# K's and Q's weights loaded in four blocks of 2 KB pieces, and the first products taken block by block

## The chip, the cores and the metric

The kernel runs on one core of one Trainium2 chip. Its engines are TensorE (PE in the profile; its weight loads have a row of their own, PEld), VectorE (DVE), ScalarE (ACT), GpSimd (POOL) and SyncE (SP), which here only issues DMAs. The metric is device time in microseconds for one execution. A median over runs is given, and beside it one execution that was taken apart by the profiler.

## The reference

The input x has 2048 rows (tokens) of 512 numbers in bf16. It is normalised row by row, and two blocks are added to it: a linear attention with 32 heads of 16, and a SwiGLU layer of width 1792.

```python
xn = _layernorm(x, axis=-1)
return x + _A_ref(xn, A_wqkv, A_wo) + _B_ref(xn, B_w_gate, B_w_up, B_w_down)

# A:  q, k, v from xn @ wqkv           (wqkv is 512 x 1536: q, then k, then v)
phi = lambda t: jnp.where(t > 0, t + 1, jnp.exp(t)) + 1e-6
pq, pk = phi(q), phi(k)
kv = jnp.einsum("bhsd,bhse->bhde", pk, v)
z = jnp.einsum("bhsd->bhd", pk)
num = jnp.einsum("bhqd,bhde->bhqe", pq, kv)
den = jnp.einsum("bhqd,bhd->bhq", pq, z)[..., None] + 1e-6
o = num / den                          # then o @ wo
# B:  (silu(x @ w_gate) * (x @ w_up)) @ w_down
```

The attention has no mask and sums over all tokens, so it doesn't matter which token stands in which row of a tile as long as input and output agree.

## The kernel before, in words

The 2048 tokens are cut into 16 tiles of 128. A small class collects the instructions of each engine in a list, in the order in which the code calls them, and works out the waits from the names of what each reads and writes (`_Prog`, L25 on). So the order of work is written out by hand: each engine goes through its list strictly in the order of the calls. A DMA stands in the list of the engine that issues it, SP or ACT. One wait holds up everything behind it on that engine. Every DMA has a semaphore of its own.

The stages are these. First the tiles are normalised and K and Q are computed (`proj_part`, `proj_first`, `proj`), with phi on ACT and DVE. V is never computed: TensorE accumulates xn-transposed times phi(K) in four banks of its output memory over all tiles (`gtacc`, L620). Then comes the SwiGLU layer in 56 steps (`ffn`), with the attention's small products in between, and then, tile by tile, the output products (`out_mm`), one addition and the store.

The change touches the first ten microseconds. There the order is this:

- `fill` (L267, called L644 and L645) has TensorE multiply constants until the first x tile is there.
- The loads: x tiles by `xload` (L204), K's and Q's weights by `wqkv_load` (L210). The weight matrix has 512 rows, loaded as four blocks c = 0 to 3 of 128 rows, one row in each partition. K's part of a row is 512 numbers, 1 KB, and Q's another 1 KB right ahead of it. One call loads one block (or two) of K or of Q. Calls L250 to L262: SP issues x 0, K 0 and 1, K 2, x 2, Q 0, Q 1, x 3, Q 2, Q 3, x 4, x 5, x 6 and 7; ACT issues x 1 (L240) and K 3.
- `rows` (L199) says which rows of x make a tile. The first `NLONE` tiles are 128 rows following each other, one per partition. The rest are dealt out so that each partition holds neighbouring rows; a load of two such tiles then has pieces of 2 KB.
- Tiles 0 to 3 don't wait for the variance. Their rows less the mean (`xc_half`, `xc_act`, `xc_add`, `xc_full`: L377 to L430) are transposed and multiplied, and the scale `rstd` is applied to the product. Tiles 0, 1 and 2 are transposed on TensorE (`tp_block` L407, `tp_first` L439) and copied out of its output memory by ACT or DVE (`tc_block` L416, `tc_first` L452). Tile 3 goes by a transposing DMA (`transpose_xc`, L432), as do the later tiles (`transpose_dma`, L460).
- `proj_part(t, wname, c, pos)` (L495) is one matmul: block c of tile t times block c of K's or Q's weights. `pos` is its place among the four that add up to one result; the first starts the sum, the fourth ends it. It waits for the tile's block and for the weights' block c. `proj_first` (L481) does two blocks in one call.
- K of a tile that is complete goes to ACT: `first_ek` (L554, an exponential) and `first_pk` (L560, the positive part). DVE clips the exponential (`clip_k`, L592), and POOL or DVE adds the two (`feat_pool` L578, `first_feat` L585). Q goes through `first_pq` (L572).

K of tile t uses bank 2 * (t % 2), Q the bank after it, so tile 2's K product must wait until ACT has read tile 0's K, tile 2's Q until ACT has read tile 0's Q, and tile 3's until ACT has read tile 1's.

The order of the calls is in L644 to L768. Around the change TensorE's list is: transposes of tiles 0 and 1; K of tile 0 (blocks 0, 1, 3, 2); K of tile 1 (the same); Q of tile 1, blocks 0 and 1; Q of tile 0, blocks 0 and 1; transposes of tile 2; Q's blocks 2 and 3 for both tiles; then K and Q of tile 2, `gtacc(0)`, and tile 3. DVE's list from L668 on: statistics of tile 2, its two halves less the mean, statistics of tile 3, `clip_k(0)`, `xc_full(3)`, statistics of tiles 4, 5 and 6, `clip_k(1)`, `xn(4)`. SP's list behind the first loads: `transpose_xc(3)`, x 8 and 9, x 10 and 11, and then the transpose of tile 4.

Of the kernel before, what the change touches and what calls it, by code (L numbers as in the profile page):

```python
# [10 lines left out]
P = 128  # L11
S = 2048
D = 512
# [96 lines left out]
def bass_parallel_sum__linear_attn_block__swiglu_ffn__prompt_kernel(  # L110
# [12 lines left out]
    K = _Prog()  # L123
    pe, act, dve, pool, sp = nc.tensor, nc.scalar, nc.vector, nc.gpsimd, nc.sync
    bf, f32 = dt.bfloat16, dt.float32

    with contextlib.ExitStack() as es:
        E = es.enter_context

        def sb(name, shape, d=bf):  # L130
            return E(nc.sbuf_tensor(name, [P] + shape, d))
# [7 lines left out]
        wqkv_sb = sb("wqkv_sb", [NDC, 3 * D])  # L139
# [52 lines left out]
        def bk(i):  # L192
            return ("bank", i)

        NLONE = 6

        def rows(v, t0, n):  # L199
            if t0 < NLONE:  # L200
                return v[t0 * P:(t0 + n) * P, :].rearrange("(t p) d -> p t d", p=P)
            return v[NLONE * P:, :].rearrange("(p t) d -> p t d", t=NT - NLONE)[:, t0 - NLONE:t0 - NLONE + n, :]

        def xload(eng, h, t0, n, after=()):  # L204
            K.dma(
                eng, lambda: h.dma_start(x_sb[:, t0:t0 + n, :], rows(xin, t0, n)),
                r=list(after), w=[("x", t0 + i) for i in range(n)],
            )

        def wqkv_load(eng, h, name, i, c0, n, after=()):  # L210
            K.dma(
                eng,
                lambda: h.dma_start(
                    wqkv_sb[:, c0:c0 + n, i * D:(i + 1) * D],
                    A_wqkv[c0 * P:(c0 + n) * P, i * D:(i + 1) * D].rearrange("(c p) f -> p c f", p=P),
                ),
                r=list(after), w=[(name, c) for c in range(c0, c0 + n)],
            )

        def wload(eng, h, name, dst, src):  # L220
# [27 lines left out]
        )  # L248

        xload("sp", sp, 0, 1)  # L250
        wqkv_load("sp", sp, "wk", 1, 0, 2)
        wqkv_load("act", act, "wk", 1, 3, 1)
        wqkv_load("sp", sp, "wk", 1, 2, 1)
        xload("sp", sp, 2, 1)
        wqkv_load("sp", sp, "wq", 0, 0, 1)
        wqkv_load("sp", sp, "wq", 0, 1, 1)
        xload("sp", sp, 3, 1)
        wqkv_load("sp", sp, "wq", 0, 2, 1)
        wqkv_load("sp", sp, "wq", 0, 3, 1)
        xload("sp", sp, 4, 1)  # L260
        xload("sp", sp, 5, 1)
        xload("sp", sp, 6, 2)  # L262

        cw = nc.const_aps.tensor(1.0, (P, P), bf)
# [33 lines left out]
        def bns(t):  # L298
            K.op("dve", lambda: dve.bn_stats(stats[:, t, :], x_sb[:, t, :]), r=[("x", t)], w=[("st", t)])  # L299
# [23 lines left out]
        def eps(t, eng):  # L323
            h = dve if eng == "dve" else pool
            K.op(
                eng,
                lambda: h.tensor_scalar(
                    out=vpe[:, t:t + 1], in0=mv[:, t, 1:2], scalar1=1e-5, scalar2=None, op0=ALU.add,
                ),
                r=[("mv", t)], w=[("vpe", t)],  # L330
            )

        def rstd_of(t):
            K.op(
                "pool",
                lambda: pool.tensor_tensor(out=rstd[:, t:t + 1], in0=vpe[:, t:t + 1], in1=nhalf[:, 0:1], op=ALU.pow),
                r=[("vpe", t), ("nhalf",)], w=[("rstd", t)],
            )
# [93 lines left out]
        def transpose_xc(t):  # L432
            K.dma(
                "sp",
                lambda: sp.dma_start_transpose(out=xcT[:, NDC * t:NDC * (t + 1), :], in_=xc_sb[:, t, :]),
                r=[("xc", t, 0), ("xc", t, 1)], w=[("xcT", t, c) for c in range(NDC)],
            )

        def tp_first(t, h, b):  # L439
            tb = banks[b].bitcast(bf)[:, 0:HD].rearrange("p (c s) -> p c s", c=2)  # L440
            K.op(
                "pe",
                [
                    (lambda c=c: pe.transpose(  # L444
                        tb[:, c, :], xc_sb[:, t, (2 * h + c) * P:(2 * h + c + 1) * P], ident[:, :],
                    ))
                    for c in range(2)
                ],
                r=[("xc", t, h), ("ident",)], w=[bk(b)],
            )  # L450

        def tc_first(t, h, b):  # L452
            tb = banks[b].bitcast(bf)[:, 0:HD].rearrange("p (c s) -> p c s", c=2)
            K.op(
                "act",
                lambda: act.activation(xcT[:, NDC * t + 2 * h:NDC * t + 2 * h + 2, :], tb, ACT.Copy),
                r=[bk(b)], w=[("xcT", t, 2 * h), ("xcT", t, 2 * h + 1)],
            )
# [36 lines left out]
        def proj_part(t, wname, c, pos):  # L495
            lo, b = (D, kb(t)) if wname == "wk" else (0, qb(t))
            K.op(
                "pe",
                lambda: pe.matmul(  # L499
                    banks[b], xcT[:, NDC * t + c, :], wqkv_sb[:, c, lo:lo + D],  # L500
                    start=(pos == 0), stop=(pos == NDC - 1),
                ),
                r=[("xcT", t, c), (wname, c)], w=[bk(b)],
            )

        def kb(t):
            return 2 * (t % 2)

        def qb(t):
            return 2 * (t % 2) + 1  # L510
# [43 lines left out]
        def first_ek(t):  # L554
            K.op(
                "act", lambda: act.activation(ek[:, t % NE, :], banks[kb(t)], ACT.Exp, scale=rstd[:, t:t + 1]),
                r=[bk(kb(t)), ("rstd", t)], w=[("ek", t % NE)],
            )

        def first_pk(t):  # L560
            K.op(
                "act", lambda: act.activation(kpos[:, t % NE, :], banks[kb(t)], ACT.Relu, scale=rstd[:, t:t + 1]),
                r=[bk(kb(t)), ("rstd", t)], w=[("kpos", t % NE)],
            )
# [90 lines left out]
        tc_block(0, 0, 4, "dve")  # L655
        tc_block(0, 1, 5, "act")
        tp_first(0, 1, 6)
        tc_first(0, 1, 6)
        eps(0, "pool")
        tp_first(1, 0, 7)  # L660
        tp_first(1, 1, 3)
        tc_first(1, 0, 7)
        bns(1)
        rstd_of(0)
        xn_dve(0)
# [7 lines left out]
        agg(3)  # L673
        proj_part(0, "wk", 0, 0)
        proj_part(0, "wk", 1, 1)
        proj_part(0, "wk", 3, 2)
        proj_part(0, "wk", 2, 3)
        first_ek(0)
        clip_k(0)
        xc_full(3)  # L680
        bns(4)
        proj_part(1, "wk", 0, 0)
        proj_part(1, "wk", 1, 1)
        proj_part(1, "wk", 3, 2)
        proj_part(1, "wk", 2, 3)
        proj_part(1, "wq", 0, 0)
        proj_part(1, "wq", 1, 1)
        transpose_xc(3)
        xload("sp", sp, 8, 2)
        xload("sp", sp, 10, 2)  # L690
        proj_part(0, "wq", 0, 0)
        proj_part(0, "wq", 1, 1)
        first_pk(0)
        tp_first(2, 0, 4)
        tc_first(2, 0, 4)
# [428 lines left out]
```

## Time and profile before

| what | value |
|---|---|
| median of 3 runs | 210.37 us (210.27 to 211.07) |
| the profiled execution, device time | 210.88 us |
| its span in the profile | 209.6 us |
| moved by DMA | 16.84 MB, mean 80 GB/s |
| busiest engine after TensorE | DVE, 57% of the span |

The profile has one row for each group of instructions: start, time from the first start to the last end, engine, line of the kernel, operation, what is written from what, the count, and in brackets how long the engine stood idle before and what released it. A table by stretches gives for each stretch its length and each engine's busy time in it with the number of instructions (x...), in the order PE, PEld, DVE, ACT, POOL; then the granted clock of TensorE, the busy share of the DMA engines, and GB/s. The granted clock stands at 1.00 in all of them here; the beat at which matmuls start is a finer measure. A matmul's row is longer than the beat, because matmuls overlap.

### The profile page before, as it was taken

The numbers are of one execution on the slowest core, as the hardware profiler recorded it, in microseconds if no ns is written. First come the engines' busy times: TensorE is split into PE (matmuls) and PEld (weight loads), VectorE is DVE, ScalarE is ACT, GpSimd is POOL, SyncE is SP. The second block draws the span as 40 slices with busy tenths as digits, with TensorE's granted clock in tenths as the row PEclk, the third lists the DMA queues.
The fourth block names the chain that finished last, engine by engine and source line by source line (L and its number), as shares of the span: only waits on it lengthen the run. The fifth ranks groups of instructions, "written<-read, shape, count | busy, mean of one in ns | idle before, by whom it ended". The sixth has DMA issues, their size and how long they took to land.

```text
span 209.6 us, 2822 instructions
## 1 busy us (share of the span) xinstructions
PE 206.9 (99%) x1014; PEld 94.5 (45%) x1014; DVE 120.3 (57%) x246; ACT 71.3 (34%) x126; POOL 72.0 (34%) x90
## 2 busy tenths in 40 slices
PE   8999999999999999999999999999999999999996
PEld 3444444444444444444444444444444444444444
DVE  4989989335465874637355746365556535374122
ACT  6686666976543331302122312213031213121000
POOL 3526977658032443223141422240424132221200
DMA  6763644697797021010101110102011010110101
GB/s 201 225 179 71 127 78 100 175 377 240 192 359 68 2 46 26 29 25 25 50 2 50 28 25 25 50 0 53 2 48 25 27 28 25 46 32 25 50 28 50
DMA packets 30287, 16.84 MB, mean 80 GB/s; under 512 B 20928, under 2 KB 29632, under 8 KB 30272
## 3 DMA queue, kind: packets, MB, share of 16 engines
q1 hardware_dynamic: 29984, 16.39, 29.9%
q10 hardware_dynamic: 288, 0.26, 0.4%
q8 instruction: 8, 0.13, 0.3%
q14 instruction: 7, 0.06, 0.1%
HBM read 9.70 MB, written 2.10 MB: 56 GB/s over the span
## 4 chain that ended last, share of the span: by engine, by line
PE 97%; DMA 1%; DVE 1%; issue 0%
PE psum L821 46%; PE psum L1026 23%; PE psum L472 10%; PE psum L1015 7%; PE psum L624 7%; PE psum L499 2%; PE psum L486 2%; DMA x_sb<-in_A_x_dram 1%; PE psum L444 0%; DVE stats L299 0%; PE psum L928 0%; PE psum L410 0%; PE psum L951 0%; DVE xc_sb L380 0%; DVE out_sb L1039 0%
## 5 line engine op out<-in xcount | busy, mean ns | idle before, releaser
L836 ACT ACTIVATE sg<-psum 128x512 bf16<-128x512 f32 x56 | 33.4, 598 | 106.0 <-PE psum L821 103.6
L821 PE MATMUL psum<-xnT,wg_sb 128*128 128x512 bf16 x224 | 57.5, 379 | 0.0
L821 PE MATMUL psum<-xnT,wu_sb 128*128 128x512 bf16 x224 | 57.5, 379 | 0.0
L970 POOL TENSOR_TENSOR prod<-pkq,zb 128x512 f32<-128x512 bf16 x16 | 18.6, 1161 | 55.9 <-DVE pkq L548 55.9
L821 PEld LDWEIGHTS psum<-xnT,wu_sb 128*128 128x128 bf16 x224 | 21.9, 98 | 26.4
L821 PEld LDWEIGHTS psum<-xnT,wg_sb 128*128 128x128 bf16 x224 | 21.7, 98 | 26.2 <-issue 0.2
L1039 DVE TENSOR_TENSOR out_sb<-psum,x_sb 128x512 bf16<-128x512 f32 (+2 forms) x17 | 11.2, 660 | 35.9 <-PE psum L1026 35.9
L994 POOL TENSOR_TENSOR pqn<-pkq,rden 128x512 bf16<-128x512 bf16 x16 | 16.9, 1055 | 36.6 <-DVE rden L988 36.6
L842 DVE TENSOR_TENSOR pkq<-psum,sg 128x512 bf16<-128x512 f32 x28 | 19.2, 686 | 17.1 <-PE psum L821 14.7
L842 DVE TENSOR_TENSOR xn_sb<-psum,sg 128x512 bf16<-128x512 f32 x28 | 18.8, 671 | 14.2 <-PE psum L821 13.6
L1026 PE MATMUL psum<-wd_sb,xn_sb 128*128 128x512 bf16 (+2 forms) x126 | 25.7, 355 | 0.0
L1026 PE MATMUL psum<-wd_sb,pkq 128*128 128x512 bf16 x112 | 25.5, 379 | 0.0
L472 PE MATMUL psum<-wqkv_sb,xnT 128*128 128x512 bf16 x96 | 22.5, 379 | 0.0
L616 POOL TENSOR_TENSOR zacc<-zacc,pkq 128x512 f32<-128x512 f32 x15 | 17.3, 1155 | 5.0 <-DVE ek L539 4.6
L1026 PEld LDWEIGHTS psum<-wd_sb,xn_sb 128*128 128x128 bf16 x126 | 11.8, 98 | 12.5
L1026 PEld LDWEIGHTS psum<-wd_sb,pkq 128*128 128x128 bf16 x112 | 11.0, 98 | 13.2
L1015 PE MATMUL psum<-m_sb,eq 128*128 128x512 bf16 (+2 forms) x68 | 16.6, 366 | 0.0
L624 PE MATMUL psum<-pkq,xn_sb 128*128 128x512 bf16 x64 | 15.9, 379 | 0.0
L472 PEld LDWEIGHTS psum<-wqkv_sb,xnT 128*128 128x128 bf16 x96 | 9.4, 98 | 11.3
L978 DVE TENSOR_REDUCE den<-prod 128x32 f32<-128x512 f32 x16 | 10.9, 683 | 5.9 <-POOL prod L970 5.9
L299 DVE BATCH_NORM_STATS2 stats<-x_sb 128x6 f32<-128x512 bf16 x16 | 10.9, 679 | 3.3 <-DMA x_sb<-in_A_x_dram 3.3
L548 DVE SCALAR_TENSOR_TENSOR pkq<-pkq,eq 128x512 bf16<-128x512 bf16 x16 | 11.1, 693 | 0.6
(73 smaller groups left out, 139.3 us busy)
## 6 DMA issues: line engine op xcount, KB each, us to landing
out_dram<-out_sb SPq DMA_DIRECT2D x15, 128.0 KB, 1.7
wg_sb<-in_B_w_gate_dram SPq DMA_DIRECT2D x2, 896.0 KB, 8.2
wu_sb<-in_B_w_up_dram SPq DMA_DIRECT2D x2, 896.0 KB, 6.4
wd_sb<-in_B_w_down_dram SPq DMA_DIRECT2D x1, 1792.0 KB, 11.1
x_sb<-in_A_x_dram SPq DMA_DIRECT2D x5, 256.0 KB, 3.0
x_sb<-in_A_x_dram SPq DMA_DIRECT2D x5, 128.0 KB, 3.2
wqkv_sb<-in_A_wqkv_dram SPq DMA_DIRECT2D x5, 128.0 KB, 3.4
wqkv_sb<-in_A_wqkv_dram SPq DMA_DIRECT2D x1, 512.0 KB, 8.4
```

The lines of the kernel that those rows point to most:

```text
L472: (lambda c=c: pe.matmul(banks[b], xnT[:, c, t * P:(t + 1) * P], wqkv_sb[:, c, lo:lo + D], start=(c == 0), stop=(c == NDC - 1),))
L548: lambda: dve.scalar_tensor_tensor(out=dst, in0=src, scalar=0.0, in1=e, op0=ALU.max, op1=ALU.add,),
L616: lambda: pool.tensor_tensor(out=zacc[:, :], in0=zacc[:, :], in1=pk, op=ALU.add),
L624: (lambda c=c: pe.matmul(banks[4 + c], xn_sb[:, t, c * P:(c + 1) * P], pkq[:, t, 0, :], start=(t == 0), stop=(t == NT - 1),))
L821: (lambda c=c: pe.matmul(banks[b], w_sb[:, c, fc * P:(fc + 1) * P], xnT[:, c, C * 512:(C + 1) * 512], start=(c == 0), stop=(c == NDC - 1),))
L836: lambda: act.activation(sg[:, j % NSG, :], banks[gb], ACT.Silu),
L842: lambda: dve.tensor_tensor(out=hT(C, fc), in0=banks[ub], in1=sg[:, j % NSG, :], op=ALU.mult,),
L970: lambda: pool.tensor_tensor(out=p, in0=pkq[:, t, 1, :], in1=zb[:, :], op=ALU.mult),
L994: lambda: pool.tensor_tensor(out=pqn[:, t % NPN, :].rearrange("p (i g h e) -> p g i h e", i=NB, g=NG, e=DH), in0=pkq[:, t, 1, :].rearrange ...
L1015: (lambda g=g: pe.matmul(dst, pqnT(t)[:, g, :], m_sb[:, g, lo:hi], start=(g == 0), stop=False,))
L1026: (lambda fc=fc: pe.matmul(dst, hT(C, fc)[:, jj * P:(jj + 1) * P], wd_sb[:, fc, lo:hi], start=False, stop=(fc == NFC - 1),))
L1039: lambda: dve.tensor_tensor(out=o, in0=src, in1=x_sb[:, t, lo:hi], op=ALU.add),
```

## The change

K's and Q's weights of one block of rows lie side by side, so one load now takes both: 128 rows with pieces of 2 KB. There are four such loads in place of seven. Block 1 is issued by ACT, the others by SP. `NLONE` goes from 6 to 4, so x tiles 4 and 5 have the dealt-out rows, and one load takes both. Tiles 0 and 1 now take their products block by block: K for both tiles and Q for tile 0 with blocks 0 and 1, then K for both with blocks 2 and 3; Q of tile 1 with blocks 0 and 1 comes after that. So the K result of tile 0 is complete after nine products and not after four, that of tile 1 after ten and not after eight. `transpose_xc(3)` and the loads of x 8 to 11 keep their places in SP's list. The copy `tc_first(0, 1)` goes behind `tc_first(1, 0)` in ACT's list.

```diff
-        NLONE = 6
+        NLONE = 4
...
+        def qk_load(eng, h, c):
+            K.dma(
+                eng,
+                lambda: h.dma_start(wqkv_sb[:, c, 0:2 * D], A_wqkv[c * P:(c + 1) * P, 0:2 * D]),
+                w=[("wk", c), ("wq", c)],
+            )
...
         xload("sp", sp, 0, 1)
-        wqkv_load("sp", sp, "wk", 1, 0, 2)
-        wqkv_load("act", act, "wk", 1, 3, 1)
-        wqkv_load("sp", sp, "wk", 1, 2, 1)
+        qk_load("sp", sp, 0)
+        qk_load("act", act, 1)
         xload("sp", sp, 2, 1)
-        wqkv_load("sp", sp, "wq", 0, 0, 1)
-        wqkv_load("sp", sp, "wq", 0, 1, 1)
+        qk_load("sp", sp, 2)
+        qk_load("sp", sp, 3)
         xload("sp", sp, 3, 1)
-        wqkv_load("sp", sp, "wq", 0, 2, 1)
-        wqkv_load("sp", sp, "wq", 0, 3, 1)
-        xload("sp", sp, 4, 1)
-        xload("sp", sp, 5, 1)
+        xload("sp", sp, 4, 2)
         xload("sp", sp, 6, 2)
...
-        tc_first(0, 1, 6)
         eps(0, "pool")
         tp_first(1, 0, 7)
         tp_first(1, 1, 3)
         tc_first(1, 0, 7)
+        tc_first(0, 1, 6)
...
         proj_part(0, "wk", 0, 0)
         proj_part(0, "wk", 1, 1)
-        proj_part(0, "wk", 3, 2)
-        proj_part(0, "wk", 2, 3)
+        proj_part(1, "wk", 0, 0)
+        proj_part(1, "wk", 1, 1)
+        proj_part(0, "wq", 0, 0)
+        proj_part(0, "wq", 1, 1)
+        proj_part(0, "wk", 2, 2)
+        proj_part(1, "wk", 2, 2)
+        proj_part(0, "wk", 3, 3)
+        proj_part(1, "wk", 3, 3)
         first_ek(0)
         clip_k(0)
         xc_full(3)
         bns(4)
-        proj_part(1, "wk", 0, 0)
-        proj_part(1, "wk", 1, 1)
-        proj_part(1, "wk", 3, 2)
-        proj_part(1, "wk", 2, 3)
-        proj_part(1, "wq", 0, 0)
-        proj_part(1, "wq", 1, 1)
         transpose_xc(3)
         xload("sp", sp, 8, 2)
         xload("sp", sp, 10, 2)
-        proj_part(0, "wq", 0, 0)
-        proj_part(0, "wq", 1, 1)
+        proj_part(1, "wq", 0, 0)
+        proj_part(1, "wq", 1, 1)
         first_pk(0)
```

## The prediction, as it was made before the changed kernel ran

> **What bounds the kernel now.** I read the page's first lines, then the busy time by stretches, then the timeline of the first 16 us for one engine after another, and last the landing times of single loads.
>
> ```profile
> span 209.6 us, 2822 instructions
> PE 206.9 (99%) x1014; PEld 94.5 (45%) x1014; DVE 120.3 (57%) x246; ACT 71.3 (34%) x126; POOL 72.0 (34%) x90
> ```
>
> ```profile
> 4.30:20.00 15.70, 15.70 (x77) 7.53 (x78) 14.41 (x42) 11.47 (x23) 7.48 (x13) 1.00 0.63 171
> 20.00:207.90 187.90, 187.78 (x931) 85.95 (x928) 104.39 (x202) 57.33 (x99) 63.40 (x69) 1.00 0.27 71
> ```
>
> Behind each stretch stand its length and then TensorE's busy time: 15.70 of 15.70, 187.78 of 187.90. From 4.3 us to 207.9 us TensorE has no hole worth naming. Before that it runs products on constants until x tile 0 is there, which the change leaves alone, and behind it comes the last output. So there is no wait on the path that this change could take away: every product it moves is already covered, in this execution. What it can do is open a hole. A hole of 0.1 us in TensorE costs 0.1 us of the end.
>
> How fast the products go is the second thing to see, in the rows of TensorE and of its weight loads:
>
> ```profile
> 0.84 3.36 PE L271 MATMUL psum<-const-bfloat16-1.0 128*128 128x512 bf16 x8 [0.84 <-PEq L1109]
> 4.26 0.40 PE L410 MATMUL psum<-ident,xc_sb 128*128 128x128 bf16 x2
> ...
> 5.09 3.52 PE L499 MATMUL psum<-wqkv_sb,xcT 128*128 128x512 bf16 x12
> 5.95 0.15 PEld L499 LDWEIGHTS psum<-wqkv_sb,xcT 128*128 128x128 bf16 x1 [0.28 <-issue]
> 6.37 0.15 PEld L499 LDWEIGHTS psum<-wqkv_sb,xcT 128*128 128x128 bf16 x1 [0.27 <-issue]
> 6.72 1.39 PEld L499 LDWEIGHTS psum<-wqkv_sb,xcT 128*128 128x128 bf16 x7 [0.20 <-issue]
> ```
>
> A weight load starts with the product ahead of its own, so these starts give the beat: 0.42 us from 5.95 to 6.37 (the eight products on constants: 3.36 us, 0.42 each), then 7 of them in 1.39 us, (1.39 - 0.10) / 6 = 0.215 us. TensorE goes at half speed until about 6.5 us, and at full speed after it. The first product starts at 5.09, so the starts of the first twelve are 5.09, 5.52, 5.95, 6.37, 6.72 and then 0.215 apart: 6.93, 7.15, 7.37, 7.58, 7.80, 8.01, 8.23 (the last ends at 5.09 + 3.52 = 8.61, so 0.38 after its start). The change keeps this beat as long as nothing is late; it puts other products into the places.
>
> **Step 1, the loads.** Removed: seven K and Q loads in 1 KB pieces and two x loads of one tile each. Added: four loads of 256 KB in 2 KB pieces and one x load of two tiles, so SP issues 8 instead of 12 loads, ACT 2 as before. The bytes stay the same, and their order decides. Landing times of before, in three answers on the line that issues them (first and last issue, then the time from issue to landing):
>
> ```profile
> L213 ACTq DMA_DIRECT2D wqkv_sb<-in_A_wqkv_dram x1: 451/451/451, 1.6 to 1.6; - x1
> L213 SPq DMA_DIRECT2D wqkv_sb<-in_A_wqkv_dram x1: 459/459/459, 1.7 to 1.7; - x1
> ...
> DMA to landing us min/median/max: 3.4/3.4/3.4
> ```
>
> ```profile
> L213 SPq DMA_DIRECT2D wqkv_sb<-in_A_wqkv_dram x2: 432/432/432, 2.7 to 3.2; - x2
> DMA to landing us min/median/max: 3.0/3.0/3.1
> ```
>
> ```profile
> L213 SPq DMA_DIRECT2D wqkv_sb<-in_A_wqkv_dram x2: 443/448/452, 4.1 to 4.6; - x2
> ...
> DMA to landing us min/median/max: 3.6/3.7/3.7
> ```
>
> ```profile
> 3.00:6.00 3.00, 2.94 (x15) 1.35 (x14) 2.93 (x10) 2.38 (x7) 0.96 (x2) 1.00 1.01 337
> 6.00:7.40 1.40, 1.40 (x7) 0.58 (x6) 1.33 (x5) 0.48 (x1) 0.62 (x2) 1.00 0.86 183
> 11.60:12.80 1.20, 1.20 (x8) 0.52 (x6) 1.20 (x5) 1.20 (x3) 0.69 (x1) 1.00 1.01 377
> ```
>
> The last two columns of the stretches are the busy share of the DMA engines and GB/s: from 3 to 6 us they are full, so a load lands when the bytes ahead of it are through. Counted in 128 KB: wk's block 2 (issued 1.7) was the sixth and landed at 1.7 + 3.4 = 5.1; wq's block 1 the ninth, 3.2 + 3.0 = 6.2; wq's block 2 the eleventh, 4.1 + 3.6 = 7.7. In the new order the first two blocks are complete with the sixth, the third with the ninth, the fourth with the eleventh. At the pace of before they land at 5.1, 6.2 and 7.7 us. They can be earlier: the 7.7 has the slow stretch in it (183 GB/s from 6.0 to 7.4), and 2 KB pieces went at 377 GB/s at 11.6 to 12.8 us (x tiles 8 to 11) against 337. Without the slow stretch the fourth lands two units after the ninth, 6.2 + 0.26 / 0.377 = 6.9 us. The second block, alone on ACT's queue, is the uncertain one: its forerunner of half the size landed at 1.6 + 3.4 = 5.0, and 131 KB more at half the rate (337 / 2) are 0.78 us, so 5.0 to 5.8.
>
> Needed: a weight load takes 0.10 us (1.39 us less six beats), so a block must be there 0.1 us before its product. The second block: second product, 5.42. The third: seventh product, 7.05. The fourth: ninth, 7.48. So the third has 0.85 us to spare. The fourth is between 0.6 early and 0.2 late. The second is between 0.4 early and 0.4 late, and a wait there falls into the slow beat, where 0.4 us hold only one product, so it costs about half, 0.2, if the speed changes at the same moment. I take nothing for both, since the nearest rows (5.1 for six units; 377 GB/s for such pieces) have them in time; the ends kept for the range are 0 and 0.2 + 0.2 = 0.4 us. A gain is excluded: TensorE has no hole to fill.
>
> **Step 2, the order of the products.** On ACT the copy of tile 1's first half goes ahead of that of tile 0's second half.
>
> ```profile
> 4.91 0.94 ACT L456 ACTIVATE xcT<-psum 128x256 bf16<-128x256 bf16 x3
> 6.92 0.69 ACT L556 ACTIVATE ek<-psum,rstd 128x512 bf16<-128x512 f32 x1 [1.08 <-PE psum L499]
> 7.50 0.68 ACT L562 ACTIVATE kpos<-psum,rstd 128x512 f32<-128x512 f32 x1
> 8.76 0.66 ACT L456 ACTIVATE xcT<-psum 128x256 bf16<-128x256 bf16 x2 [0.57 <-PE psum L444]
> 9.52 0.69 ACT L574 ACTIVATE pkq<-psum,rstd 128x512 bf16<-128x512 f32 x1
> 10.10 0.68 ACT L556 ACTIVATE ek<-psum,rstd 128x512 bf16<-128x512 f32 x1
> 11.24 0.70 ACT L562 ACTIVATE kpos<-psum,rstd 128x512 f32<-128x512 f32 x1
> ```
>
> The first row's three copies are done by 5.85 (against two in 0.66 below, so one every 0.28, each 0.38 long); the third product, at 5.95, needs the copy that stood second and ended at 4.91 + 0.28 + 0.38 = 5.57, and that now goes first: hidden. The real edit is later. K of tile 0 was complete after the fourth product and `first_ek(0)` began at 6.92; now it is complete after the ninth, which ends as the trace's products do 0.38 after its start (7.58 + 0.38), so `first_ek(0)` begins at 8.00, 1.08 us later. ACT had 1.08 us of idle time ahead of it and 0.57 behind `first_pk(0)`; the second is what pays. ACT's chain from 8.00, at the spacing of the rows (0.58, then (11.24 - 10.10) / 2 = 0.57): `first_pk(0)` 8.58, tile 2's copies 9.15 to 9.81 (the first done at 9.15 + 0.38 = 9.53), `first_pq(0)` 9.71 to 10.40, `first_ek(1)` 10.28, `first_pq(1)` 10.85, `first_pk(1)` 11.42 to 12.12. TensorE waits for three of these:
>
> ```profile
> 9.53 1.89 PE L486 MATMUL psum<-wqkv_sb,xcT 128*128 128x512 bf16 x8
> 10.26 0.67 PEld L486 LDWEIGHTS psum<-wqkv_sb,xcT 128*128 128x128 bf16 x4 [0.19 <-ACT pkq L574]
> 11.99 1.53 PEld L486 LDWEIGHTS psum<-wqkv_sb,xcT 128*128 128x128 bf16 x8 [0.20 <-ACT kpos L562]
> ```
>
> Before, a weight load that waited for ACT came 0.05 us after ACT's end (9.52 + 0.69 = 10.21 to 10.26; 11.24 + 0.70 = 11.94 to 11.99). Tile 2's K product stood at 9.53; its weight load now starts at 9.53 + 0.05 and takes 0.10, so the product starts at 9.68: **0.15 us late**. Tile 2's Q: 10.40 + 0.15 = 10.55, due at 10.40 (four products after 9.53) + 0.15 = 10.55: nothing more. Tile 3: 12.12 + 0.15 = 12.27, due at 12.12 + 0.15: nothing more. The three agree, so the step costs 0.15; its ends are 0 (if ACT's copies go 0.15 sooner) and 0.3 (twice the distance). It moves with step 1: what makes the ninth product late moves both sides alike.
>
> **Step 3, what queues behind the waiting clip on DVE.** `clip_k(0)` waits for `first_ek(0)`, and behind it in DVE's order stand `xc_full(3)`, the statistics of tiles 4 to 6 and `xn(4)`.
>
> ```profile
> 7.87 0.26 DVE L539 TENSOR_SCALAR ek<-ek 128x512 bf16<-128x512 bf16 x1
> 8.04 0.35 DVE L426 TENSOR_SCALAR xc_sb<-x_sb,mv 128x512 bf16<-128x512 bf16 x1
> 8.69 0.69 DVE L299 BATCH_NORM_STATS2 stats<-x_sb 128x6 f32<-128x512 bf16 x1 [0.30 <-DMA x_sb<-in_A_x_dram]
> 11.28 0.73 DVE L316 TENSOR_SCALAR xn_sb<-x_sb,mv,rstd 128x512 bf16<-128x512 bf16 x2
> 8.42 1.28 SPq L435 DMA_TRANSPOSE xcT<-xc_sb  x1
> 11.71 1.19 SPq L463 DMA_TRANSPOSE xnT<-xn_sb  x1
> 8.28 1.16 POOL L581 TENSOR_TENSOR pkq<-kpos,ek 128x512 bf16<-128x512 f32 x1 [0.45 <-ACT kpos L562]
> 15.36 1.61 PEld L472 LDWEIGHTS psum<-wqkv_sb,xnT 128*128 128x128 bf16 x8
> ```
>
> ```profile
> xnT<-xn_sb SPq DMA_TRANSPOSE x16, 2.5
> ...
> xcT<-xc_sb SPq DMA_TRANSPOSE x1, 2.5
> ```
>
> The clip moves from 7.87 to 8.00 + 0.69 + 0.03 = 8.72, so `xc_full(3)` ends at 8.72 + 0.17 + 0.35 = 9.24 and its transpose issues at 9.27 instead of 8.42. With 2.5 us to landing it is there at 11.8, while tile 3's first weight load starts at 11.99. The statistics start at 9.25 instead of 8.69, 0.56 later, so `xn(4)` goes from 11.28 to 11.84, its transpose from 11.71 to 12.27 and at 2.5 us to landing lands by 14.8; the product that reads it loads weights at 15.36 + 0.15. Slack 0.2 and 0.7 us, so the cost is nothing; if this cover is gone it is one for one. The x loads of tiles 8 to 11, behind the transpose on SP, go 0.85 later and are needed on DVE only behind `xn(4)` to `xn(6)`. POOL's `feat_pool(0)` starts 1.1 later, ends near 10.5, and the product that reads it starts eight beats after 9.53, at 11.26. The new row layout of tiles 4 and 5 leaves their stores at 1 KB pieces.
>
> **The sum.** 0 + 0.15 + 0 = 0.15 us. This execution took 210.88 us (209.6 of span and 1.28 around it), so its like would take 211.03. The median of the runs shown is 210.37, 0.51 under it; the difference is carried over: 210.37 + 0.15 = **210.5 us**. From 0 to 0.4 + 0.3 the bounds give 210.4 to 211.1. Less than about 0.5%, 1.05 us, this measurement can't tell from no change.
>
> **The rivals.**
> (a) The late blocks bite: the second 0.4 late (0.2 us), the fourth 0.2 late, step 2 as worked: 210.37 + 0.55 = 210.9, up to 211.1. For it: six units landed only at 5.1, and the slow stretch from 6.0 to 7.4. Against: 2 KB pieces and four issues fewer.
> (b) Slower, by one mechanism: the wait for the second block on ACT's queue, if it lands after 5.42, breaks the work that brings TensorE to full speed. It was at half speed from 0.84 to about 6.5, 5.7 us, with a hole of 0.06 (4.20 to 4.26). If a hole at 5.4 starts that count anew, it stays slow until 5.4 + 5.7 = 11.1, 4.6 us longer, of which half is lost: 2.3 us, 212.7. If it counts only in part, half of this, 211.6. Against: the hole would be 0.4 us at most, and the trace doesn't show whether one that short counts.
> [...]
> (c) Slightly faster: in executions that reach full speed at 5.1 already, the twelve products and the transposes end 0.85 earlier (four beats of 0.215). Then before waits for its last block (4.6 + 3.7 = 8.3; its product stands two beats ahead of 9.53 and would come at 8.25, so 0.15 late), and the change, whose last block is there by 6.9, does not: 210.2.
> (d) Faster by over 1.05 us would need a hole of that size that this trace doesn't have.
>
> **How the numbers follow.** Forecast (210.3 to 210.7) 0.57; (a) 0.20; (b) 0.10; (c) 0.10; (d) 0.03. The cases without (b) and (d) reach from 210.2 (c) to 211.1 (a); the runs shown lie 0.80 apart (210.27 to 211.07), and for a quarter of that I go to 210.0 and 211.3. This holds the forecast, (a) and most of (c). Faster by over 0.5%: (d), 0.03. Slower: (b), 0.10. Within: 0.87.
>
> **What would show it.** Step 1: no idle time at products two and nine, landings near 5.1, 6.2 and 6.9 to 7.7. Step 2: `first_ek(0)` at about 8.0, and a hole of 0.15 in TensorE at about 9.6. Step 3: `clip_k(0)` at 8.7, both transposes landed before their readers. Wrong would be: a second block after 5.42 with the slow beat going on beyond 7 us; a hole at 15.4 us (step 3); or a span under 209 us.

## The result, and the profile after

| | median | lowest to highest | executions |
|---|---|---|---|
| before | 210.39 us | 210.01 to 211.07 | 22 |
| changed | 211.22 us | 210.49 to 213.45 | 22 |

The ratio, changed to before, is 1.0056, 95% interval 1.0031 to 1.0080: slower by about 0.6%, between 0.65 and 1.7 us. 0.15 us was forecast. The highest values say most: six of the changed kernel's 22 executions lie between 212.6 and 213.5 us, none of before's. The other sixteen have a mean of 211.06 us, 0.6 above before's mean of 210.47.

The profiled execution of the changed kernel took 210.49 us, the lowest of its 22 and less than the 210.88 of the one shown for before. So these two traces can't simply be subtracted. First the timeline of TensorE and ACT at the start, changed kernel:

```profile
span 209.3 us, 2800 instructions
```

```profile
4.64 0.28 ACT L422 ACTIVATE xcT<-psum 128x128 bf16<-128x128 bf16 x1
4.96 0.38 PE L502 MATMUL psum<-wqkv_sb,xcT 128*128 128x512 bf16 x1
5.61 2.07 PEld L502 LDWEIGHTS psum<-wqkv_sb,xcT 128*128 128x128 bf16 x11 [0.59 <-ACT xcT L459]
5.64 2.53 PE L502 MATMUL psum<-wqkv_sb,xcT 128*128 128x512 bf16 x11 [0.31 <-ACT xcT L459]
7.57 0.69 ACT L559 ACTIVATE ek<-psum,rstd 128x512 bf16<-128x512 f32 x1 [1.67 <-PE psum L502]
8.24 1.03 PE L502 MATMUL psum<-wqkv_sb,xcT 128*128 128x512 bf16 x4
9.16 0.11 PEld L489 LDWEIGHTS psum<-wqkv_sb,xcT 128*128 128x128 bf16 x2 [0.39 <-ACT xcT L459]
9.16 1.90 PE L489 MATMUL psum<-wqkv_sb,xcT 128*128 128x512 bf16 x8
15.00 1.61 PEld L475 LDWEIGHTS psum<-wqkv_sb,xnT 128*128 128x128 bf16 x8
```

Eleven products in 2.53 us are (2.53 - 0.38) / 10 = 0.215 us each: this execution was at full speed at 5 us already, the one shown for before only at 6.5. And there is a hole. The first product starts at 4.96, the second at 5.64 and not 0.215 later: 0.47 us lost. The profile names a copy by ACT, but the copy that the second product needs (L422) was over at 4.92. A product with several waits is put down to the one that the profile sees end last, and here it was the load of block 1 (the loads under issue from 1.5 to 1.6 us, SP's block 0 and ACT's block 1, and their landing times):

```profile
L223 SPq DMA_DIRECT2D wqkv_sb<-in_A_wqkv_dram x1: 412/412/412, 1.3 to 1.3; - x1
L223 ACTq DMA_DIRECT2D wqkv_sb<-in_A_wqkv_dram x1: 450/450/450, 1.6 to 1.6; - x1
...
DMA to landing us min/median/max: 3.0/3.5/4.0
```

Block 0 landed at 1.3 + 3.0, about 4.2 us, and block 1 at 1.6 + 4.0, about 5.5 us (the addends are rounded). The weight load of the second product followed at 5.61. In the other traces with a hole at this product it starts about 0.1 us after block 1's landing too, whatever the profile names: at 5.96 for about 5.9 us in the repeat, at 6.45 for 6.35 with block 1 on SP, at 6.71 for 6.6 with the short bridge.

### The profile page after: what moved, and what is told of

Same layout as the page of the kernel before. It is cut to its first block, busy times and chain, and to the rows that moved or that the text cites. A ratio compares the mean times of both kernels' runs of the same rounds, so it can differ in the third digit from the quotient of the medians.

```text
span 209.3 us, 2800 instructions
## 1 busy us (share of the span) xinstructions
PE 205.0 (98%) x995; PEld 93.8 (45%) x1014; DVE 120.1 (57%) x246; ACT 71.1 (34%) x126; POOL 72.1 (34%) x90
## 4 chain that ended last, share of the span: by engine, by line
PE 96%; DVE 1%; DMA 1%; issue 1%; ACT 0%
PE psum L824 46%; PE psum L1029 23%; PE psum L475 10%; PE psum L1018 7%; PE psum L627 6%; PE psum L489 2%; PE psum L502 2%; DMA x_sb<-in_A_x_dram 1%; DVE stats L302 0%; DVE pkq L551 0%; PE psum L931 0%; ACT xcT L459 0%; PE psum L447 0%; PE psum L954 0%; DVE xc_sb L383 0%
## 5 line engine op out<-in xcount | busy, mean ns | idle before, releaser
L824 PE MATMUL psum<-xnT,wu_sb 128*128 128x512 bf16 x216 | 55.8, 379 | 0.4
```

The lines of the kernel that those rows point to most:

```text
L824: (lambda c=c: pe.matmul(banks[b], w_sb[:, c, fc * P:(fc + 1) * P], xnT[:, c, C * 512:(C + 1) * 512], start=(c == 0), stop=(c == NDC - 1),))
```

## The experiments

Two theories stood against each other. T1: block 1 lands late, the second product waits, and in part of the executions that hole also takes away full speed. T2: the price is step 2 of the prediction, the later `first_ek(0)` and ACT's chain behind it. A third, T3, puts it on x tiles 4 and 5. Each run was timed beside the kernel before on the same chip; before's medians there were 210.31 to 210.44.

| run | median | lowest to highest | ratio to before (95%) |
|---|---|---|---|
| order alone | 210.72 | 210.25 to 211.05 | 1.0010 (1.0000 to 1.0019) |
| block 1 on SP | 210.99 | 210.62 to 211.43 | 1.0028 (1.0017 to 1.0040) |
| bridge | 210.95 | 210.78 to 211.61 | 1.0029 (1.0016 to 1.0041) |
| x 4 and 5 alone | 210.76 | 210.54 to 211.18 | 1.0014 (1.0005 to 1.0022) |
| changed, again | 211.48 | 210.38 to 213.32 | 1.0051 (1.0027 to 1.0076) |
| changed without x 4 and 5 | 211.43 | 210.81 to 213.44 | 1.0036 (1.0009 to 1.0062) |
| K's blocks 0 and 1 first | 210.74 | 210.34 to 211.76 | 1.0018 (1.0003 to 1.0033) |
| block 1 last | 214.38 | 213.75 to 216.33 | 1.0213 (1.0178 to 1.0247) |
| block 1 last, bridge | 212.92 | 212.55 to 213.68 | 1.0129 (1.0109 to 1.0149) |
| x 4 and 5, one load, old layout | 210.43 | 210.01 to 211.00 | 1.0005 (0.9993 to 1.0017) |
| new layout, two loads | 210.33 | 209.99 to 210.94 | 0.9997 (0.9985 to 1.0010) |
| rest later | 211.49 | 211.00 to 211.68 | 1.0054 (1.0034 to 1.0073) |
| x 2 behind | 211.62 | 211.35 to 214.02 | 1.0092 (1.0048 to 1.0136) |
| K and Q apart | 211.11 | 210.77 to 211.51 | 1.0037 (1.0023 to 1.0050) |

### The order alone

The changed order of products and copies over the loads of before.

```diff
-        NLONE = 4
+        NLONE = 6
...
-        qk_load("sp", sp, 0)
-        qk_load("act", act, 1)
+        wqkv_load("sp", sp, "wk", 1, 0, 2)
+        wqkv_load("act", act, "wk", 1, 3, 1)
...
```

> The changed order of products and copies, with the loads and the row layout of before. Theory T1 (the second block, alone on ACT's queue, lands at 5.5 us and holds up the second product; in part of the executions that hole also delays full speed): here K's blocks 0 and 1 land by 4.3 us, so no hole at the second product, no execution above 212.5 us, median within 0.2 of before (210.3 to 210.6). T2 (the price is the later first_ek and ACT's chain behind it): the price stays, median 210.8 to 211.2.

Measured: a ratio of 1.0010, 0 to 0.4 us, nothing above 211.05. The median of 210.72 lies between the two ranges, 0.12 above T1's and 0.08 below T2's; that no execution is high goes with T1. So the order may cost a few tenths, and the trace shows a small part of it:

```profile
5.12 3.13 PE L506 MATMUL psum<-wqkv_sb,xcT 128*128 128x512 bf16 x12
8.31 1.03 PE L506 MATMUL psum<-wqkv_sb,xcT 128*128 128x512 bf16 x4
9.23 0.11 PEld L493 LDWEIGHTS psum<-wqkv_sb,xcT 128*128 128x128 bf16 x2 [0.39 <-ACT xcT L463]
```

All twelve first products run in one piece. Behind the four products from 8.31 on the next one was due at 8.31 + 4 * 0.215 = 9.17. Tile 2's first weight load and product wait for ACT's copy until 9.23, as step 2 said: a hole of 0.06 us. The changed kernel has the same one (8.24 and 9.16).

### Block 1 on SP

```diff
-        qk_load("act", act, 1)
+        qk_load("sp", sp, 1)
```

> The changed kernel with the load of block 1 issued by SP right behind block 0 instead of by ACT. T1: SP issues it 0.2 later, but it no longer shares the DMA engines with what SP queued behind it, so it lands at 4.9 to 5.2 us, the hole shrinks to 0.2 us or less, hardly any execution above 212.5, median 210.4 to 210.8. T2: no change, median 210.9 to 211.4 with the same tail to 213. If block 1 lands at 5.5 again, the bytes ahead of it decide and not the queue, and the time stays that of the changed kernel.

Measured: 210.99, in T2's range by the median, and nothing above 211.43, as T1 has it. The trace goes against T1's reason for the run: TensorE waited longer, not less, and this time the profile names the load.

```profile
5.16 0.38 PE L502 MATMUL psum<-wqkv_sb,xcT 128*128 128x512 bf16 x1
6.48 2.63 PE L502 MATMUL psum<-wqkv_sb,xcT 128*128 128x512 bf16 x11 [0.94 <-DMA wqkv_sb<-in_A_wqkv_dram]
```

The second product started 1.32 us after the first, and block 1 landed at 6.3. So ACT's queue is not what makes block 1 late. That none of the ten executions is high proves little: the changed kernel has eight above 212.5 in the 34 executions of its two runs, and at this rate ten without one come by chance about once in 15.

### A bridge of products over the hole

```diff
         proj_part(0, "wk", 0, 0)
+        bridge(2)
         proj_part(0, "wk", 1, 1)
```

`bridge(n)` has TensorE multiply constants n times into the bank that tile 1's K overwrites later.

> The changed kernel with two more products on constants (into a bank that is overwritten) between the first and the second product, so that TensorE works while block 1 is on its way. They add 0.43 us of work at full speed and 0.85 at half speed. T1 with the clock: the hole is gone, so no execution above 212.5 us; the median is at that of the changed kernel or up to 0.4 above it (211.0 to 211.6). If the executions near 213 have nothing to do with the hole, about a quarter of them stay there, and the highest reach 213.5.

Measured: 210.95, just under T1's range, and nothing above 211.61 in 10 executions, which alone could again be chance. Two more products, 0.43 us of work at full speed, made the kernel no slower than it was (211.22): they stood in time that was idle. Block 1 landed at 6.6 in this trace, so 0.92 us were still lost behind the bridge.

### X tiles 4 and 5 alone

The kernel before with `NLONE = 4` and one load for x tiles 4 and 5.

> The kernel before with only the other part of the change: x tiles 4 and 5 in one load and the row layout from tile 4 on. T1 and T2 both: nothing on the path waits for these tiles (transposes land 0.7 us or more before their readers), so 210.2 to 210.6, no execution above 211.2. A third theory, that the new layout of tiles 4 and 5 or the earlier loads behind them cost the time, has 210.9 or more here.

Measured: 1.0014, so 0.1 to 0.5 us that neither T1 nor T2 has. The median of 210.76 lies between their 210.6 and T3's 210.9, a point for T3 in kind and not in size. The trace of this run is that of its highest execution, 211.18 us (TensorE, then DVE, then the weight loads):

```profile
8.32 0.61 PE L498 MATMUL psum<-wqkv_sb,xcT 128*128 128x512 bf16 x2 [0.29 <-DMA wqkv_sb<-in_A_wqkv_dram]
9.24 0.60 PE L498 MATMUL psum<-wqkv_sb,xcT 128*128 128x512 bf16 x2 [0.31 <-DMA wqkv_sb<-in_A_wqkv_dram]
```

```profile
9.92 0.69 DVE L298 BATCH_NORM_STATS2 stats<-x_sb 128x6 f32<-128x512 bf16 x1 [1.48 <-DMA x_sb<-in_A_x_dram]
```

```profile
15.02 0.55 PEld L623 LDWEIGHTS psum<-pkq,xn_sb 128*128 128x128 bf16 x4 [0.49 <-DVE pkq L587]
```

The largest loss is at Q's blocks 2 and 3. Their four products were due from 7.86 on, and TensorE waits for the two loads: 0.46 and 0.49 us are lost. The blocks landed at 8.3 and 9.2 us, in the trace shown for before at 7.7 and 8.3. DVE waits 1.48 us for tile 4 (0.30 there), and the wait for DVE at 15 us costs TensorE 0.17 us. The load of x 3 is late too, 7.1 for 6.5 us; whether the load of x 4 and 5 behind it does all this, one trace can't tell. In the changed kernel all of Q is there by 6.9 us, so it has no such wait. Two later runs took the part in two: one load in the old layout, and the new layout with two loads.

> The kernel before with x tiles 4 and 5 in one load, but in the row layout of before (two pieces of 1 KB per partition). T3a (tile 4's statistics now wait until tile 5 is there too, and DVE is the next engine to hold up TensorE): 210.6 to 210.9 as with the whole x part. T3b (the new layout costs): 210.3 to 210.5.

> The kernel before with the new row layout from tile 4 on, but tiles 4 and 5 loaded one by one (1 KB pieces 12 KB apart). T3a (one load for two tiles costs): 210.3 to 210.5, as before. T3b (the layout costs): 210.6 to 210.9.

Neither costs anything that shows (1.0005 and 0.9997, both intervals across 1). So T3a and T3b both miss. The part cost only as a whole, and why stays open.

### The changed kernel again, and without x 4 and 5

> The changed kernel again, on the chip of the runs beside it. T1 (block 1's late landing opens a hole at the second product, and the hole delays full speed in some executions): the same spread as before, from 210.5 to over 212.5 in about a quarter of the executions, median 210.9 to 211.3, and a hole of 0.3 us or more at the second product in its trace. If the times above 212.5 came from the chip and not from the kernel, there are none here.

Measured: 211.48, a little above the range, two of 12 executions above 212.5, on the chip where most runs had none. So the chip is not the reason. Its trace has the hole too, 5.99 - 4.97 - 0.215 = 0.80 us:

```profile
4.97 0.38 PE L502 MATMUL psum<-wqkv_sb,xcT 128*128 128x512 bf16 x1
5.99 2.53 PE L502 MATMUL psum<-wqkv_sb,xcT 128*128 128x512 bf16 x11 [0.64 <-ACT xcT L459]
```

Beside it ran the changed kernel with `NLONE = 6` and x tiles 4 and 5 one by one.

> The changed kernel with x tiles 4 and 5 loaded one by one and the row layout of before: the four weight blocks and the order of products alone. T1: the hole at the second product stays, and with it the executions above 212.5 and a median of 210.8 to 211.2. T3 (tiles 4 and 5 in one load cost 0.35 us, as in the kernel before with that alone, and independently of the rest): median 0.35 below the changed kernel's.

Measured: 211.43, above T1's range, one of 12 above 212.5. The hole and the high times don't come from x 4 and 5; a share of 0.35 in the rest can't be told in such a spread. The profiled execution was the one at 213.44 us, and it shows what goes with such a time. First TensorE and its weight loads, then two stretches (the last three columns: granted clock, DMA share, GB/s):

```profile
4.95 0.38 PE L503 MATMUL psum<-wqkv_sb,xcT 128*128 128x512 bf16 x1
6.97 4.22 PE L503 MATMUL psum<-wqkv_sb,xcT 128*128 128x512 bf16 x11 [1.64 <-DMA wqkv_sb<-in_A_wqkv_dram]
11.02 0.39 PE L448 MATMUL psum<-ident,xc_sb 128*128 128x128 bf16 x4
```

```profile
6.93 0.59 PEld L503 LDWEIGHTS psum<-wqkv_sb,xcT 128*128 128x128 bf16 x4 [1.92 <-issue]
7.80 0.15 PEld L503 LDWEIGHTS psum<-wqkv_sb,xcT 128*128 128x128 bf16 x1 [0.28 <-issue]
8.23 0.15 PEld L503 LDWEIGHTS psum<-wqkv_sb,xcT 128*128 128x128 bf16 x1 [0.28 <-issue]
```

```profile
5.00:7.00 2.00, 0.36 (x3) 0.08 (x3) 0.81 (x3) 0.90 (x3) 0.07 (x1) 1.00 1.02 346
7.40:10.80 3.40, 3.40 (x10) 1.16 (x9) 1.89 (x6) 0.62 (x2) 1.04 (x2) 0.50 0.35 127
```

TensorE was at full speed before the hole (0.38 us for the first product; in the trace shown for before, at half speed, it lasted 0.63). The hole is 6.97 - 4.95 - 0.215 = 1.80 us, and the profile counts TensorE as idle for 1.64 of it. After it the beat is fast for a moment (four weight loads in 0.59 us), and from 7.4 to 10.8 us the granted clock is 0.50 and a product takes 0.43. 3.4 us at half speed are 1.7 us lost; with the 1.80 that is about 3.5 us, and the execution lies 3.0 above before's median (the executions of before have a spread of their own). The mean granted clock of the execution is 0.992; four of the six high times of the 22, and one of the two of the repeat, have the same figure. The other three (212.63, 212.74 and 213.14) have 1.0 and no trace, so what made them high is not shown.

### K's blocks 0 and 1 first

```diff
-        qk_load("sp", sp, 0)
-        qk_load("act", act, 1)
+        wqkv_load("sp", sp, "wk", 1, 0, 2)
+        wqkv_load("act", act, "wq", 0, 0, 2)
```

> The changed kernel with its first two blocks loaded as K's blocks 0 and 1 in one load on SP and Q's blocks 0 and 1 in one load on ACT (1 KB pieces), the rest as changed, so 256 KB and not 512 stand ahead of the second product. T1: no hole at the second product (the load lands by 4.3 us), no execution above 212.5, median 210.5 to 210.8, what is left above before being the x tiles' part. T2 (ACT's chain after the ninth product): no change against the changed kernel, 210.9 to 211.3.

Measured: 210.74 and nothing above 211.76, as T1 has it and T2 has not. Its trace shows the limit of such a repair:

```profile
4.93 1.06 PE L502 MATMUL psum<-wqkv_sb,xcT 128*128 128x512 bf16 x4
7.17 1.90 PE L502 MATMUL psum<-wqkv_sb,xcT 128*128 128x512 bf16 x8 [1.19 <-DMA wqkv_sb<-in_A_wqkv_dram]
```

Four products run without a wait, K's blocks 0 and 1 of two tiles. The fifth, Q's, waits for the load on ACT's queue. The hole is smaller in most executions, going by the times, not gone.

### Block 1 last, without and with a bridge

The cause enlarged: SP issues block 1 behind block 3. The second run puts `bridge(8)` into the wait.

```diff
-        qk_load("act", act, 1)
         xload("sp", sp, 2, 1)
         qk_load("sp", sp, 2)
         qk_load("sp", sp, 3)
+        qk_load("sp", sp, 1)
```

> The changed kernel with the cause enlarged: block 1 is issued by SP behind block 3, so it lands at about 7 us in every execution and the second product waits some 1.8 us, as in the one execution whose trace showed the lower clock. T1 (a hole of this length takes TensorE back to half speed, or keeps it there): most executions show it, median 212.3 to 213.6, mean granted clock about 0.992 in at least half of those at full speed before the hole. If only the wait itself counts: 1.8 less the 0.4 of the changed kernel, median 212.2 to 212.8, clock 1.0, no execution above 213.

> The same late block 1, with eight products on constants (into a bank that is overwritten) between the first and the second product: 1.73 us of work at full speed, 3.4 us at half speed. T1: no lowered clock in any execution and none of the times near 213.5 that go with it; the wait is as long as before, so 212.0 to 212.6 where full speed came early, up to 213 where it came late. If the lower clock has another cause than an idle TensorE, it appears here as often as in the run without the bridge.

Measured: 214.38 without, 212.92 with the bridge. Mean granted clock: 0.992 or below in five of six executions without it, 1.0 in all five with it. Without the bridge, TensorE and two stretches:

```profile
5.02 0.54 PE L502 MATMUL psum<-wqkv_sb,xcT 128*128 128x512 bf16 x1
7.71 3.87 PE L502 MATMUL psum<-wqkv_sb,xcT 128*128 128x512 bf16 x11 [2.15 <-DMA wqkv_sb<-in_A_wqkv_dram]
```

```profile
9.00:10.00 1.00, 1.00 (x4) 0.30 (x2) 0.00 (x0) 0.00 (x0) 0.00 (x0) 0.50 0.00 0
10.00:11.00 1.00, 1.00 (x4) 0.35 (x3) 0.00 (x0) 0.66 (x2) 0.00 (x0) 0.50 0.00 0
```

With the bridge:

```profile
5.44 1.94 PE L284 MATMUL psum<-const-bfloat16-1.0 128*128 128x512 bf16 x8
8.07 2.53 PE L512 MATMUL psum<-wqkv_sb,xcT 128*128 128x512 bf16 x11 [0.69 <-DMA wqkv_sb<-in_A_wqkv_dram]
```

```profile
9.00:10.00 1.00, 1.00 (x6) 0.42 (x5) 0.20 (x2) 0.01 (x1) 0.00 (x0) 1.00 0.01 4
```

The block was no earlier with the bridge (the next product starts at 8.07, without it at 7.71), and yet the kernel is 1.5 us faster, with eight products more to do. So here the lowered clock goes with the idleness and not with the wait: after 2.15 us idle the granted clock was 0.50 from 9 to 11 us, after 0.69 us idle it was 1.00, and the wait was no shorter. The run without the bridge came out above its range, and the one with it (212.92) between 212.6 and 213, where executions were expected that reach full speed late. In the two traces the block landed at 7.6 and 7.9 and not at 7.

### Why block 1 is late

Three more runs went to the step that had failed. First, the loads behind block 1 held back: SP issues x 2 and all that follows only after tile 0's mean.

```diff
+        bns(0)
+        agg(0)
+        xload("sp", sp, 2, 1, [("mv", 0)])
+        qk_load("sp", sp, 2)
+        qk_load("sp", sp, 3)
...
```

> The changed kernel with SP's loads from x 2 on issued only after tile 0's mean (about 3.9 us instead of 1.7), so that only 768 KB are on the way until 5 us. H1 (what is queued behind takes the DMA engines from block 1): block 1 lands by 4.9 us, no hole of 0.3 us at the second product; later holes instead, since block 2 comes at 6.5 to 7. H2 (the slow stretch of the DMA engines comes by itself, whatever is queued): block 1 lands at 5.4 or later in this trace too.

```profile
4.95 1.47 PE L496 MATMUL psum<-wqkv_sb,xcT 128*128 128x512 bf16 x6
7.19 1.73 PE L496 MATMUL psum<-wqkv_sb,xcT 128*128 128x512 bf16 x6 [0.77 <-DMA wqkv_sb<-in_A_wqkv_dram]
```

```profile
L223 ACTq DMA_DIRECT2D wqkv_sb<-in_A_wqkv_dram x1: 450/450/450, 1.6 to 1.6; - x1
...
DMA to landing us min/median/max: 2.8/3.1/3.5
```

Block 1 landed at 1.6 + 3.5 = 5.0 to 5.1, where the prediction had put it, and the first six products ran in one piece. That is 0.1 above H1's mark, and well under the 5.4 of H2. The price comes later: block 2 is now the one waited for, at the seventh product, and the time is no better (211.49). What the DMA engines had moved by the landing of block 1 differs much (last figure: GB/s from the start), in the changed kernel's first trace and in this one:

```profile
0.00:5.50 5.50, 4.30 (x17) 1.57 (x17) 2.40 (x8) 3.54 (x8) 1.74 (x10) 1.00 0.69 218
0.00:5.00 5.00, 4.06 (x17) 1.57 (x17) 1.93 (x7) 3.05 (x7) 1.69 (x10) 1.00 0.50 159
```

That is 1.20 MB against 0.80. The two x tiles and blocks 0 and 1 make 0.79 MB. So in the changed kernel 0.4 MB of later loads had come in before block 1 was complete.

The traces also hold the 16 steps in which the semaphore of a load rises, and the landing is the last of them. In the changed kernel's first trace 13 of block 1's 16 steps came by 4.77 us, and the last three at 5.08, 5.37 and 5.51. With block 1 on SP twelve came by 4.90, and the last two at 6.11 and 6.35. With the rest later, 15 came by 4.78 and the last at 5.02. So most of block 1 is there in time in these three, and a few late parts decide. In the repeat of the changed kernel more of it is late: eight of the 16 steps came after 5.1. The tail is shortest where nothing is queued behind, but that is one trace, and what holds these parts up is not shown.

Second, only x 2 behind block 3.

> The changed kernel with the load of x 2 behind block 3 on SP. H1 with x 2's 1 KB pieces as what takes the turn: block 1 lands 0.3 us earlier than in the changed kernel (5.2), median 210.7 to 211.0. H2: no difference, 5.5 or later, median 211.0 to 211.6.

```profile
5.06 0.38 PE L502 MATMUL psum<-wqkv_sb,xcT 128*128 128x512 bf16 x1
6.29 2.53 PE L502 MATMUL psum<-wqkv_sb,xcT 128*128 128x512 bf16 x11 [0.85 <-DMA wqkv_sb<-in_A_wqkv_dram]
```

No help, as H2 has it: the second product comes 1.23 us after the first, two of six executions are at 213 and above, and the median of 211.62 is even higher. So x 2 is not what delays block 1; blocks 2 and 3 are still queued behind it. Third, K and Q of each block as two loads of 1 KB pieces.

> The changed kernel with each block as two loads of 1 KB pieces, K's first, on the same queue, so the second product waits for K's 128 KB of block 1 only. T1: K's part lands by 5.0 us (as the 128 KB on ACT's queue did in the kernel before), the hole is 0.2 us or less, nothing above 212.5, median 210.5 to 210.8. If 2 KB pieces or the queue are the cause, block 1's K part is no earlier than 5.4 here or the hole stays.

```profile
4.94 0.38 PE L506 MATMUL psum<-wqkv_sb,xcT 128*128 128x512 bf16 x1
5.74 2.85 PE L506 MATMUL psum<-wqkv_sb,xcT 128*128 128x512 bf16 x11 [0.42 <-ACT xcT L463]
```

```profile
3.50:4.50 1.00, 0.95 (x6) 0.19 (x5) 0.93 (x5) 0.97 (x3) 0.46 (x2) 1.00 0.58 142
```

Nothing above 211.51, but 211.11 and a hole of 5.74 - 4.94 - 0.215 = 0.59. T1 misses: K's half of block 1 alone landed at 5.6, no earlier than the whole block in the changed kernel's first trace. And since the hole is there with 1 KB pieces, pieces of 2 KB are not what it takes. The last row shows the other part: from 3.5 to 4.5 us the DMA engines moved 142 GB/s in this trace, against 348 in the changed kernel's first one. The same stretch of time shows 160 GB/s with the short bridge, 187 without x 4 and 5, and 277 in the repeat. A slow stretch isn't needed for a late block 1: the changed kernel's first trace had none before 5.5 us, and with x 2 behind the rate from 3.5 to 4.5 us was 307 GB/s. In the trace shown for before it came at 6.0 to 7.4, when all of K was in. What brings it on stays open.

## Why the prediction was wrong, point by point

**That TensorE has no hole, so nothing is to be gained:** right. No version here beat the kernel before.

**Step 1, the landing of the second block: this failed.** It was put at 5.0 to 5.8 us, taken as in time, and its worst price set at 0.2 us. Measured were 5.5 and about 5.9 in the two traces of the changed kernel and 6.6 with the short bridge, and holes of 0.47 and 0.80 us in the former and of 1.80 us without x 4 and 5. Three things were wrong in the step. It counted the bytes ahead of the block as if a load landed when these are through. With nothing queued behind, 768 KB did land by 5.1 us (rest later); in the changed kernel the last parts of block 1 came after 0.4 MB of later loads. It took the slow stretch from the one trace at hand as if it always came after 6 us. And it set the deadline at 5.42 by that trace's slow beat, while at full speed the second product is due 0.215 after the first, at about 5.17.

**The third and fourth blocks:** the landings are right, 6.1 and 6.9 us in the first trace for 6.2 and 6.9 to 7.7. That no product waits for them, in either trace of the changed kernel, is luck for the fourth: without the hole the ninth product would have been due at 4.96 + 8 * 0.215 = 6.68, before the landing at 6.9. With block 1 on SP and with K and Q apart, the ninth product did wait for block 3.

**Step 2, ACT's chain:** right in kind. 0.15 us was forecast for the wait of tile 2's first product for ACT's copy; it measured 0.06 us, in the order alone and in the changed kernel. The order alone costs 0 to 0.4 us by its interval, and what makes up the rest of that isn't shown.

**Step 3, DVE's order and the transposes:** right, no wait at tile 4's product (15.00 in the first trace). That x 4 and 5 cost nothing is not borne out for the kernel before, where as a whole they cost 0.1 to 0.5 us; in the changed kernel no cost of theirs can be told (211.43 without, 211.48 with them).

**Rival (b), half speed after a hole:** in kind this is what happened in part of the executions, with 0.10 given to it. There is one difference. (b) had the hole put off full speed; in the trace of 213.44 us TensorE was at full speed already and lost it behind the hole. That this goes with the idleness is shown by the bridge (granted clock 0.50 after 2.15 us idle, 1.00 after 0.69). That unbroken work is what brings full speed was the author's estimate from the 5.7 us of one trace; no run here tests it. The price of 2.3 or half of that was about right (1.7 for the slow stretch). "0.4 us at most" for the hole was the error, the same as in step 1. The lowered mean clock is there in five of 34 executions of the changed kernel, at 213.07 to 213.45. Of the kernel before one of 117 executions lies above 212.5 (212.88), with a mean clock of 1.0.

**Rival (c), executions that reach full speed early:** they exist. This is the second trace of the kernel before, TensorE and its weight loads:

> The kernel before once more, for a second trace. If the moment of full speed differs from one execution to the next, its beat changes at another time than 6.5 us, and the first twelve products end up to 0.85 us earlier or later than 8.61. T1 has no hole at the second product in it.

```profile
5.00 2.90 PE L499 MATMUL psum<-wqkv_sb,xcT 128*128 128x512 bf16 x12
7.74 0.39 PE L444 MATMUL psum<-ident,xc_sb 128*128 128x128 bf16 x4
```

```profile
5.36 1.39 PEld L499 LDWEIGHTS psum<-wqkv_sb,xcT 128*128 128x128 bf16 x7 [0.21 <-ACT xcT L456]
```

Seven weight loads in 1.39 us from 5.36 on are full speed, the twelve products end at 7.90 instead of 8.61, and the execution took 210.16 instead of 210.88. But before doesn't wait for its last block in this trace, so the change had nothing to win here. A wait of that kind did come in the trace of x 4 and 5 alone, which was fast from its first product on (twelve products in 2.75 us). The first product here shows where full speed began (duration in ns):

```profile
L499 PE MATMUL psum<-wqkv_sb,xcT x1: 527/527/527, 5.0 to 5.0; 128*128 128x512 bf16 x1
```

It took 0.53 us, between the 0.63 of half speed and the 0.38 of full speed, so by these two the change of speed fell into it. That is why the twelve products take 0.15 us more than 11 beats and 0.38; it is no wait. The changed kernel's first trace had full speed ahead of its first product. It is still 210.49 - 210.16 = 0.33 us slower, with a hole of 0.47 us that this trace doesn't have.

**The sum:** no change that can be told was forecast, and the changed kernel is slower by an interval that begins at 0.31%; its median of 211.22 lies above the sum's bounds of 210.4 to 211.1. The wider range of 210.0 to 211.3 holds it, but only by what was added for the spread of the runs. Of the 1.17 us between the means of the 22 executions, about 0.6 are in the sixteen ordinary ones, and the six high ones add as much again.

## What to carry to other kernels

Count for each early product how much must have landed before it can start, and give it slack of the size by which landing times differ between executions, not the slack of one trace. Here block 1 landed at 5.5 and 5.9 us in the two traces of one kernel, and at 6.8 without x 4 and 5. Fusing loads makes pieces larger, but it also changes what stands ahead of the first user. Before, K's blocks 0 and 1 were one load, the first of the weights, and there at 4.3 us. After it, Q's half of block 0 stood between them, and bringing K's blocks 0 and 1 first again took the hole at the second product away. A few products on constants in a long early wait were cheap here: where TensorE stood idle for 2.15 us (block 1 last), eight of them took the granted clock behind the wait from 0.50 to 1.00 and the time from 214.38 to 212.92 us.

## What the runs showed of the hardware beside that

Full speed came ahead of the first product in the changed kernel's first trace (4.96 us), at the second product in before's second (5.36), and at 6.5 us in the one shown for before, with the same work ahead of it. In the two traces of before this goes with 0.7 us of the time (210.16 and 210.88; the twelve products end at 7.90 and 8.61), more than most edits here. The beat of the first products has to be compared before two traces are.

After a hole of 1.80 us TensorE went on at full speed from 6.97 to 7.4 us and only then, for 3.4 us, at a granted clock of 0.50. The slow part comes behind the wait that it goes with, and looks like a matter of its own. Idle stretches of 0.94 us (block 1 on SP) and 1.19 us (K's blocks 0 and 1 first) left the clock at 1.00 in their traces; 1.64 and 2.15 us were followed by 0.50.
